# Where VectorE's share of the second weight matrix's conversion stands in a fused linear attention and gated feed-forward kernel

## The chip, the core and the metric

The kernel runs on one core of one Trainium2 chip. The core has five engines that work side by side, each through its own list of instructions in a fixed order: TensorE (PE in the profile; its weight loads are shown as PEld), VectorE (DVE), ScalarE (ACT), GpSimd (POOL) and SyncE (SP), which here issues all DMAs. An instruction waits until what it needs is there, and everything behind it on the same engine waits too. The metric is the time of one execution in microseconds on the device. The kernel before takes 837.52 us (median of 3 runs, 836.57 to 838.53).

## What is computed

Linear attention for 8 batches of 8 heads (576 positions, head size 64), then a gated feed-forward layer with a convolution of length 3 over the positions:

```python
def phi(x):
    proj = np.einsum('bhsd,df->bhsf', x, w_phi)
    proj = proj - np.max(np.abs(proj), axis=-1, keepdims=True)
    return np.concatenate([np.exp(proj), np.exp(-proj)], axis=-1)
q_p, k_p = (phi(q), phi(k))
kv = np.einsum('bhsf,bhsd->bhfd', k_p, v)
z = np.sum(k_p, axis=2)
num = np.einsum('bhsf,bhfd->bhsd', q_p, kv)
den = np.einsum('bhsf,bhf->bhs', q_p, z)[..., None] + 1e-06
x = num / den                                  # the heads side by side: 512 columns
h = np.maximum(x @ w_in, 0.0)                  # 512 x 1024
conv_out += conv_w[k][None, None, :] * hp[:, k:k + S, :]
gate = 1.0 / (1.0 + np.exp(-conv_out))
return (h * gate @ w_out).astype(np.float32)   # 1024 x 512
```

The inputs `w_in`, `conv_w` and `w_out` are 64-bit floats. They reach the kernel as pairs of 32-bit words and are turned into 32-bit floats on the chip.

## The kernel before

**Products in two parts.** Most matmuls work on operands split into a high part (rounded to the PE's fp32r form) and a low part (the rest), as three products: high by high, high by low, low by high. The helper `split` (L56 to L65) makes the two parts: the high part on the engine it is given, the low part by a subtraction (L65).

**The weights.** `load_weight(n)` handles tile n of 16, each 128 x 512: tiles 0 to 7 are `w_in`, 8 to 15 are `w_out`. For each, `weight_split` (L111) loads the raw words `w_r` by a DMA on SP (L120), and `float64_round` (L96) builds the 32-bit value in the temporary `w_t`: four instructions on DVE (L100, L102, L104, L107), two on ACT (L101, L106), one on POOL (L109). Then ACT makes the high part (L60) and POOL the low part (L65). `w_r` comes from a pool of two buffers with the tag `gh`, `w_t` from one of two with the tag `gl`. So tile n needs the buffers of tile n - 2, and the two parts of the gated activations, gh and gl, take the same buffers afterwards.

**Attention.** For each batch and each half of its heads (`qd`), five groups `g` of positions are worked on for k and for q. The rows of the profile follow this path: kx or qx (inputs split on POOL), kp or qp (projection on PE), km or qm (maximum) and ks or qs (difference) on DVE; for k, ke (exponentials on ACT) and kv (PE); for q, tp (transposed on PE), qe and qh (ACT), ql (DVE), nm (numerator and denominator, PE), num and dr (PSUM emptied by ACT), den and rc (reciprocal, DVE). `x_process(b, p)` then makes x for pair p of heads and half c of the positions: rb (PE spreads the reciprocals), xf (DVE), xh (ACT), xl (DVE, L65). The low part for b = 0, p = 3, c = 0 is called xl0_3_0; it is the last of the first batch's operands that the first half needs.

**Feed-forward.** Each of 16 halves n goes through `h_part` (hp on PE, L435, h on ACT), `conv_process` (c, on POOL and twice on DVE, L463; one sigmoid; a product on DVE, L471; then gh on ACT and gl on DVE) and `o_part` (op on PE, L494). The part op0_0 is the first output product: half 0, columns 0 to 127; op0_1 is the next, columns 128 to 255. Each needs gh and gl of half 0 (gh0_0 and gl0_0 hold the first half of their rows) and all eight tiles of `w_out`.

**What sets the order.** The code emits its steps from a small planner: generators that are resumed in a modelled time of their own, with `until` for what must have been emitted before. `weight_process` waits with tile 8 until x of (0, 3, 0) has been emitted. That is only the order of emission. A scheduler at build time then arranges the instructions of each engine anew, by priorities, dependences and estimated times, and may put a later one ahead where it sees the engine free. A helper `after(ins, trace)` traces a step such that each of its instructions on the engine of `ins` gets an edge to `ins`, and so can't be put ahead of it; the instructions on other engines get none.

```python
raw = sb.tile([P, 1024], I32, name=f"{name}r", tag="gh", bufs=2)
nc.sync.dma_start(out=raw, in_=src)
tmp = sb.tile([P, 2, 512], F32, name=f"{name}t", tag="gl", bufs=2)
```

Of the kernel before, what the change touches and what calls it, by code (L numbers as in the profile page):

```python
# [7 lines left out]
F32 = mybir.dt.float32  # L8
# [4 lines left out]
ALU = mybir.AluOpType  # L13
# [22 lines left out]
def kernel(  # L36
# [13 lines left out]
    nc = tc.nc  # L50
# [6 lines left out]
    def split(src, hi, lo, eng_hi, eng_lo):  # L57

        if eng_hi is nc.scalar:
            nc.scalar.activation(out=hi, in_=src, func=AF.Copy)  # L60
        elif eng_hi is nc.gpsimd:
            nc.gpsimd.tensor_scalar(out=hi, in0=src, scalar1=1.0, scalar2=0.0, op0=ALU.mult, op1=ALU.add)  # L62
        else:
            nc.vector.tensor_copy(out=hi, in_=src)
        eng_lo.tensor_tensor(out=lo, in0=src, in1=hi.bitcast(F32), op=ALU.subtract)  # L65


    def load_const(ap, shape, name):
# [7 lines left out]
    wbd_hi = cp.tile([P, 2 * F], F32R, name="wbd_hi")  # L76
    wbd_lo = cp.tile([P, 2 * F], F32R, name="wbd_lo")
    split(wbd_f, wbd_hi, wbd_lo, nc.vector, nc.vector)
    idn = load_const(ident, [P, P], "idn")

# [30 lines left out]
    def weight_split(src, n, hi, lo):  # L111

        name = f"w{n}_"
        if src.dtype == F32:
            raw = sb.tile([P, 512], F32, name=f"{name}r", tag="gh", bufs=2)
            nc.sync.dma_start(out=raw, in_=src)
            split(raw, hi, lo, nc.gpsimd, nc.gpsimd)
            return
# [3 lines that stand above are left out]
        w = tmp[:, 0, :]  # L122
        float64_round(raw, w, tmp[:, 1, :])
        split(w, hi, lo, nc.scalar, nc.gpsimd)
# [16 lines left out]
    def load_weight(n):  # L141
        if n < 8:
            c, sl = n // 2, slice((n % 2) * 512, (n % 2) * 512 + 512)
            weight_split(w_in[n], n, win_hi[c][:, sl], win_lo[c][:, sl])
        else:
            weight_split(w_out[n - 8], n, wout_hi[n - 8], wout_lo[n - 8])
# [10 lines left out]
    def pe(ns):  # L157
        return ("pe", ns)
# [4 lines left out]
    def until(*keys):  # L163
        return ("until", [k for k in keys if k is not None])

    def set_ready(key, ns=0):
        ready[key] = now[0] + ns * LAT
# [45 lines left out]
    def after(ins, trace):  # L213

        if ins is None:
            return trace()
        with tc.issue_after(ins.ins):
            return trace()
# [81 lines left out]
    den = {}  # L300
    numt = {}
    xh, xl = {}, {}

    def q_process(b, qd, g):
        j = (b * NQ + qd) * 5 + g
# [79 lines left out]
        if g == 2 or g == 4:  # L385
            spawn(x_process(b, qd * 2 + g // 2 - 1))

    def x_process(b, p):
        yield ("wait", 4000)
        qd, pr = divmod(p, 2)  # L390
        dn, nt = den[b, qd, pr], numt[b, qd, pr]
        if 4 * b + p > 0:
            yield until(("x", *divmod(4 * b + p - 1, 4), 1))
        with tc.high_priority():
            rc = sb.tile([72, 16], F32, name=f"rc{b}_{p}", tag="rc", bufs=2)
            nc.vector.tensor_scalar(out=dn, in0=dn, scalar1=1e-6, scalar2=None, op0=ALU.add)
            nc.vector.reciprocal(out=rc, in_=dn)
            rhl = [sb.tile([72, 16], F32R, name=f"rc{j}{b}_{p}", tag=f"rc{j}", bufs=2) for j in range(2)]
            split(rc, rhl[0], rhl[1], nc.vector, nc.vector)
            for j in range(2):  # L400
                for i in range(2):
                    nc.sync.dma_start(out=rr[2 * j + i : 2 * j + i + 1, :].bitcast(F32).rearrange("o (r c) -> o r c", c=16),
                                      in_=rhl[j].bitcast(F32).rearrange("(r i) c -> i r c", i=2)[i])
        yield ("wait", 4500)
        for c in range(2):
            yield until(("h", 2 * (b - 1) + c) if b > 0 else None)
            t0 = 0 if c == 0 else S - HW
            with tc.high_priority():
                rb = pg.tile([P, HW], F32, name=f"rb{b}_{p}_{c}", tag="g", bufs=4)
                nc.tensor.matmul(out=rb, lhsT=sel_r, rhs=rr[:, t0 : t0 + HW], start=True, stop=True)  # L410
                xf = sb.tile([P, HW], F32, name=f"xf{b}_{p}_{c}", tag="xf", bufs=2)
                nc.vector.tensor_tensor(out=xf, in0=nt[:, t0 : t0 + HW], in1=rb, op=ALU.mult)
                xh[b, p, c] = sb.tile([P, HW], F32R, name=f"xh{b}_{p}_{c}", tag="xh", bufs=8)
                xl[b, p, c] = sb.tile([P, HW], F32R, name=f"xl{b}_{p}_{c}", tag="xl", bufs=8)
                split(xf, xh[b, p, c], xl[b, p, c], nc.scalar, nc.vector)
            set_ready(("x", b, p, c), 2500)
            yield pe(125)

# [91 lines left out]
    def weight_process():  # L510
        for n in range(16):
            if n == 8:

                yield until(("x", 0, 3, 0))
            load_weight(n)
            yield ("wait", 4000)
            if n == 7:
                set_ready("w_in", 0)
        set_ready("w_out", 0)
# [18 lines left out]
    start = {}  # L538
    moe = [0.0, moe_process(), False, None]
    active.append([0.0, weight_process(), False, 0])  # L540

    def step(p, kind):
# [24 lines left out]
    while moe is not None or chains or active:  # L567
        while chains and sum(1 for p in active if p[2]) < WINDOW:
            b, x, g, kind = chains.pop(0)
# [3 lines left out]
            p = active[-1]  # L573
# [10 lines left out]
        if can_a and (a_first or not can_m):  # L584
            p = active[can_a[0]]
# [66 lines left out]
```

## Time and profile before

| | |
|---|---|
| median of 3 runs | 837.52 us (836.57 to 838.53) |
| the profiled execution | 838.25 us, of which 836.5 us from its first to its last instruction (the span) |
| mean granted PE clock | 0.99 of full speed |
| PE busy, share of the span | 797.7 us, 95% |
| PE weight loads | 781.0 us, 93% |
| DVE | 626.6 us, 75% |
| ACT | 572.6 us, 68% |
| POOL | 307.9 us, 37% |
| DMA | 49.19 MB, 59 GB/s on average |

Busy time is the time in which an engine has an instruction in work. The page also has the span in 40 slices of 20.9 us, with the busy share of each engine in tenths, so that 9 means 90% or more. A share over the whole span mixes stages with different limits, and the first 130 us of this kernel are unlike the rest: the weights are converted there and only attention has work for PE.

### The profile page before, as it was taken

The page shows a single profiled execution, that of the slowest core. Times are in us where ns is not written, and L with a number is a line of the kernel's source. Part 1 is how long each engine was busy: PE and PEld are TensorE (multiplying, and loading weights), DVE is VectorE, ACT ScalarE, POOL GpSimd, SP SyncE. Part 2 cuts the span into 40 slices and gives each one's busy share as a digit, 9 for nine tenths or more (in the row PEclk, how much of TensorE's full clock was granted, in tenths as well). Part 3 has the DMA queues.
Part 4 walks back from the last instruction along what each step waited for, and adds up shares of the span by engine and source line. Part 5 has one row for each costly group of instructions (what it writes and reads, how often), then busy time and mean ns, then how long its engine had stood idle before and what let it go on. Part 6 is the DMA issues. An engine that isn't in the chain of part 4 may idle for free.

```text
span 836.5 us, 18006 instructions
## 1 busy us (share of the span) xinstructions
PE 797.7 (95%) x6414; PEld 781.0 (93%) x6414; DVE 626.6 (75%) x1326; ACT 572.6 (68%) x1228; POOL 307.9 (37%) x469
## 2 busy tenths in 40 slices
PE   7888679999999999999999999999999999999998
PEld 6767579989999999999999999999999999999998
DVE  5889998899876777877677786778687776856561
ACT  4788777797767767786777867577585876744332
POOL 4657774443432433515133332434143221211110
PEclk9899999999999999999999999999999999999999
DMA  6544322111111211121121212112121100000001
GB/s 184 167 137 142 107 65 53 53 52 54 54 53 54 66 33 51 45 74 52 49 59 35 68 42 59 46 53 62 31 70 37 44 20 20 13 29 29 22 19 46
DMA packets 56337, 49.19 MB, mean 59 GB/s; under 512 B 15029, under 2 KB 54201, under 8 KB 56249
## 3 DMA queue, kind: packets, MB, share of 16 engines
q1 hardware_dynamic: 56248, 48.05, 19.8%
q8 instruction: 51, 0.84, 0.4%
q14 instruction: 38, 0.30, 0.1%
HBM read 38.14 MB, written 9.44 MB: 57 GB/s over the span
## 4 chain that ended last, share of the span: by engine, by line
PE 78%; DVE 9%; ACT 6%; DMA 3%; issue 3%; POOL 1%; SPq 0%; DVEq 0%; ACTq 0%; POOLq 0%
PE op L494 24%; PE hp L435 22%; PE nm L360 8%; PE kv L259 7%; PE tp L324 3%; PE qp L203 2%; PE qp L204 2%; PE qp L205 2%; PE kp L203 1%; PE kp L204 1%; PE kp L205 1%; PE kv L255 1%; DMA w_r<-in_w_in_dram 1%; PE nm L352 1%; PE rb L410 1%
## 5 line engine op out<-in xcount | busy, mean ns | idle before, releaser
L463 DVE SCALAR_TENSOR_TENSOR c<-h,cw,c 128x287 f32<-128x287 f32 (+1 forms) x256 | 138.6, 551 | 36.2 <-POOL c L458 34.3
L259 PE MATMUL kv<-v,ke 128*128 128x65 f32 x1024 | 161.1, 254 | 2.2 <-ACT ke L240 2.1
L259 PEld LDWEIGHTS kv<-v,ke 128*128 128x128 f32 x1024 | 155.2, 194 | 5.7 <-ACT ke L240 2.7
L435 PE MATMUL hp<-xh,win_hi 128*128 128x290 f32 x512 | 153.3, 301 | 2.9 <-ACT h L442 2.3
L458 POOL TENSOR_SCALAR c<-h,cw 128x288 f32<-128x288 f32 x128 | 76.7, 601 | 208.9 <-ACT h L442 170.9
L435 PE MATMUL hp<-xl,win_hi 128*128 128x290 f32 x512 | 153.0, 299 | 0.4 <-DVE xl L65 0.4
L435 PE MATMUL hp<-xh,win_lo 128*128 128x290 f32 x512 | 152.1, 297 | 0.0
L494 PE MATMUL op<-gh,wout_hi 128*128 128x288 f32 x512 | 152.1, 297 | 0.0
L494 PE MATMUL op<-gh,wout_lo 128*128 128x288 f32 x512 | 151.7, 296 | 0.0
L494 PE MATMUL op<-gl,wout_hi 128*128 128x288 f32 x512 | 151.6, 296 | 0.0
L62 POOL TENSOR_SCALAR kxh<-kr 128x256 fp32r<-128x256 f32 (+1 forms) x80 | 38.2, 477 | 198.5 <-PE kp L204 175.1
L65 DVE TENSOR_TENSOR ql<-qe,qh 128x512 fp32r<-128x512 f32 x112 | 81.9, 745 | 35.9 <-ACT qh L60 35.9
L435 PEld LDWEIGHTS hp<-xh,win_hi 128*128 128x128 f32 x512 | 97.2, 191 | 4.6 <-ACT h L442 3.1
L435 PEld LDWEIGHTS hp<-xl,win_hi 128*128 128x128 f32 x512 | 97.2, 190 | 1.2 <-DVE xl L65 1.2
L435 PEld LDWEIGHTS hp<-xh,win_lo 128*128 128x128 f32 x512 | 97.1, 190 | 0.0
L494 PEld LDWEIGHTS op<-gh,wout_lo 128*128 128x128 f32 x512 | 96.4, 188 | 0.0
L494 PEld LDWEIGHTS op<-gl,wout_hi 128*128 128x128 f32 x512 | 96.2, 188 | 0.0
L494 PEld LDWEIGHTS op<-gh,wout_hi 128*128 128x128 f32 x512 | 96.1, 188 | 0.0
L442 ACT ACTIVATE h<-hp 128x290 f32<-128x290 f32 x128 | 51.7, 410 | 51.9 <-PE hp L435 46.9
L378 ACT ACTIVATE dr<-nm 1x512 f32<-1x512 f32 (+1 forms) x96 | 46.3, 482 | 45.1 <-PE nm L360 23.6
L330 ACT ACTIVATE qe<-tp 128x512 f32<-128x512 f32 x112 | 61.9, 598 | 20.4 <-PE tp L324 16.5
L240 ACT ACTIVATE ke<-ks 128x512 f32<-128x512 f32 (+1 forms) x80 | 47.0, 588 | 39.1 <-DVE ks L210 38.6
(88 smaller groups left out, 2034.7 us busy)
## 6 DMA issues: line engine op xcount, KB each, us to landing
v<-in_vt_dram SPq DMA_DIRECT2D x80, 130.0 KB
out_dram<-os SPq DMA_DIRECT2D x64, 144.0 KB
qr<-in_qT_dram SPq DMA_DIRECT2D x64, 128.0 KB
kr<-in_kT_dram SPq DMA_DIRECT2D x64, 128.0 KB
w_r<-in_w_in_dram SPq DMA_DIRECT2D x8, 512.0 KB
w_r<-in_w_out_dram SPq DMA_DIRECT2D x8, 512.0 KB
rr<-rc SPq DMA_DIRECT2D x128, 2.2 KB
qr<-in_qT_dram SPq DMA_DIRECT2D x16, 64.0 KB
```

The costliest lines, as they stand in the source:

```text
L62: nc.gpsimd.tensor_scalar(out=hi, in0=src, scalar1=1.0, scalar2=0.0, op0=ALU.mult, op1=ALU.add)
L65: eng_lo.tensor_tensor(out=lo, in0=src, in1=hi.bitcast(F32), op=ALU.subtract)
L240: nc.scalar.activation(out=e[:, 0], in_=pr, func=AF.Exp)
L259: ins = nc.tensor.matmul(out=kp[i][:, s, p0 : p0 + VW], lhsT=lhsT, rhs=v[:, (2 * t + i) * VW : (2 * t + i + 1) * VW], start=False, stop=(g ...
L330: nc.scalar.activation(out=e, in_=tp.rearrange("p i t s -> p i (t s)"), func=AF.Exp, scale=1.0 - 2.0 * s)
L360: ins = after(ins, lambda: nc.tensor.matmul(out=ps[:, i, o : o + w], lhsT=w_, rhs=x_, start=(k == 0), stop=(k == 5)))
L378: nc.scalar.activation(out=dro.rearrange("o (r i c) -> o i r c", i=2, c=16), in_=ps[D : D + 1, :, o : o + w].rearrange("o i (r c) -> o i r ...
L435: nc.tensor.matmul(out=ps, lhsT=w_, rhs=x_, start=(k == 0), stop=(k == 11))
L442: nc.scalar.activation(out=hs, in_=ps, func=AF.Relu)
L458: nc.gpsimd.tensor_scalar(out=cv, in0=hs[:, o : o + TC], scalar1=cw[:, f, 1:2], scalar2=0.0, op0=ALU.mult, op1=ALU.add)
L463: nc.vector.scalar_tensor_tensor(out=cv[:, lo:hi], in0=hs[:, o + j - 1 + lo : o + j - 1 + hi], scalar=cw[:, f, j : j + 1], in1=cv[:, lo:hi ...
L494: nc.tensor.matmul(out=ps, lhsT=w_, rhs=x_, start=(k == 0), stop=(k == 23))
```

## The change

`split` returns its last instruction, the subtraction. `x_process` keeps that of each low part of x in `anchors`. `weight_process` issues tiles 8 and 9, the first two of `w_out`, through `after` with the anchor of (0, 3, 0), the instruction that makes xl0_3_0 on DVE. So the four DVE instructions of each of these two tiles may not stand ahead of xl0_3_0 on DVE. The rest of the two tiles, on ACT, POOL and SP, gets no edge; nor do tiles 10 to 15.

```diff
@@ split
-        eng_lo.tensor_tensor(out=lo, in0=src, in1=hi.bitcast(F32), op=ALU.subtract)
+        return eng_lo.tensor_tensor(out=lo, in0=src, in1=hi.bitcast(F32), op=ALU.subtract)
@@ beside xh, xl
+    anchors = {}
@@ x_process
-                split(xf, xh[b, p, c], xl[b, p, c], nc.scalar, nc.vector)
+                anchors[b, p, c] = split(xf, xh[b, p, c], xl[b, p, c], nc.scalar, nc.vector)
@@ weight_process
-            load_weight(n)
+            after(anchors[0, 3, 0] if n in (8, 9) else None, lambda: load_weight(n))
```

```python
def after(ins, trace):
    if ins is None:
        return trace()
    with tc.issue_after(ins.ins):
        return trace()
```

The scheduler arranges all engines anew with the edge in place, so the order differs from there on. In the rows below, names carry batch or half first, then the parts in the order used above (km1_0_2 is batch 1, half 0 of the heads, group 2; w8_t is the temporary of tile 8); the last number only counts tiles. Lines behind L302 are one higher in the change.

On DVE, right behind the last instruction of tile 7 (the end of `w_in`), before:

```order
L107 SCALAR_TENSOR_TENSOR w7_t_461<-w7_t_461,w7_r_459 128x512
L100 TENSOR_SCALAR w8_t_1711<-w8_r_1709 128x512
L208 TENSOR_REDUCE km1_0_1_748<-kp1_0_1_741 128x4
L210 TENSOR_TENSOR ks1_0_1_750<-kp1_0_1_741,km1_0_1_748 128x512
L396 TENSOR_SCALAR den0_0_1_499<-den0_0_1_499 72x16
L208 TENSOR_REDUCE qm0_1_3_758<-qp0_1_3_755 128x4
L102 TENSOR_SCALAR w8_t_1711<-w8_r_1709 128x512
L104 SCALAR_TENSOR_TENSOR w8_t_1711<-w8_r_1709,w8_t_1711 128x512
L397 RECIPROCAL rc0_1_934<-den0_0_1_499 72x16
L210 TENSOR_TENSOR qs0_1_3_760<-qp0_1_3_755,qm0_1_3_758 128x512
L107 SCALAR_TENSOR_TENSOR w8_t_1711<-w8_t_1711,w8_r_1709 128x512
L64 CAST rc00_1_937<-rc0_1_934 72x16
```

The same place in the change:

```order
L107 SCALAR_TENSOR_TENSOR w7_t_461<-w7_t_461,w7_r_459 128x512
L208 TENSOR_REDUCE km1_0_1_748<-kp1_0_1_741 128x4
L210 TENSOR_TENSOR ks1_0_1_750<-kp1_0_1_741,km1_0_1_748 128x512
L397 TENSOR_SCALAR den0_0_1_499<-den0_0_1_499 72x16
L208 TENSOR_REDUCE qm0_1_3_758<-qp0_1_3_755 128x4
L398 RECIPROCAL rc0_1_934<-den0_0_1_499 72x16
L210 TENSOR_TENSOR qs0_1_3_760<-qp0_1_3_755,qm0_1_3_758 128x512
L64 CAST rc00_1_937<-rc0_1_934 72x16
L65 TENSOR_TENSOR rc10_1_938<-rc0_1_934,rc00_1_937 72x16
L208 TENSOR_REDUCE km1_0_2_846<-kp1_0_2_839 128x4
L210 TENSOR_TENSOR ks1_0_2_848<-kp1_0_2_839,km1_0_2_846 128x512
L413 TENSOR_TENSOR xf0_0_0_863<-num0_0_0_494,rb0_0_0_861 128x290
```

The instructions of tiles 8 and 9 are gone from between the attention work, and xf0_0_0 follows sooner. The same holds for all rows of tiles 8 to 15 up to the anchor, 32 in all.

On DVE at the anchor, in the change (before, w14 and w15 were done by here, and no row of a weight follows):

```order
L65 TENSOR_TENSOR xl0_3_0_1459<-xf0_3_0_1456,xh0_3_0_1458 128x290
L100 TENSOR_SCALAR w8_t_1711<-w8_r_1709 128x512
L100 TENSOR_SCALAR w9_t_1803<-w9_r_1801 128x512
L210 TENSOR_TENSOR ks2_0_0_1476<-kp2_0_0_1470,km2_0_0_1474 128x256
L208 TENSOR_REDUCE qm1_1_1_1488<-qp1_1_1_1481 128x4
L208 TENSOR_REDUCE qm1_1_2_1507<-qp1_1_2_1500 128x4
L65 TENSOR_TENSOR xl0_3_1_1467<-xf0_3_1_1464,xh0_3_1_1466 128x290
L102 TENSOR_SCALAR w8_t_1711<-w8_r_1709 128x512
L104 SCALAR_TENSOR_TENSOR w8_t_1711<-w8_r_1709,w8_t_1711 128x512
L210 TENSOR_TENSOR qs1_1_1_1490<-qp1_1_1_1481,qm1_1_1_1488 128x512
L102 TENSOR_SCALAR w9_t_1803<-w9_r_1801 128x512
L104 SCALAR_TENSOR_TENSOR w9_t_1803<-w9_r_1801,w9_t_1803 128x512
```

Tiles 8 and 9 begin directly behind xl0_3_0 and go on in pairs between attention and the convolution of half 0.

On DVE ahead of the first low part of the gated activations, before:

```order
L471 TENSOR_TENSOR c0_1838<-c0_1838,h0_7_1649 128x288
L210 TENSOR_TENSOR qs2_0_2_2384<-qp2_0_2_2375,qm2_0_2_2382 128x512
L397 RECIPROCAL rc1_3_2804<-den1_1_1_1895 72x16
L65 TENSOR_TENSOR ql2_0_1_2431<-qe2_0_1_0_2432,qh2_0_1_2430 128x512
L65 TENSOR_TENSOR gl0_0_2441<-c0_1838,gh0_0_2440 128x288
L65 TENSOR_TENSOR ql2_0_1_2431<-qe2_0_1_1_2436,qh2_0_1_2430 128x512
```

and in the change, behind the last weight instruction:

```order
L65 TENSOR_TENSOR ql2_0_1_2431<-qe2_0_1_0_2432,qh2_0_1_2430 128x512
L398 RECIPROCAL rc1_3_2804<-den1_1_1_1895 72x16
L65 TENSOR_TENSOR ql2_0_1_2431<-qe2_0_1_1_2436,qh2_0_1_2430 128x512
L64 CAST rc01_3_2807<-rc1_3_2804 72x16
L208 TENSOR_REDUCE km2_1_2_2702<-kp2_1_2_2695 128x4
L65 TENSOR_TENSOR rc11_3_2808<-rc1_3_2804,rc01_3_2807 72x16
L210 TENSOR_TENSOR ks2_1_2_2704<-kp2_1_2_2695,km2_1_2_2702 128x512
L208 TENSOR_REDUCE qm2_0_3_2716<-qp2_0_3_2709 128x4
L210 TENSOR_TENSOR qs2_0_3_2718<-qp2_0_3_2709,qm2_0_3_2716 128x512
L65 TENSOR_TENSOR gl0_0_2441<-c0_1838,gh0_0_2440 128x288 x4
```

In the change the last DVE instruction of tile 15 (w15_t, L107) stands five rows ahead of the first of these rows, and seven rows of attention (the second ql2_0_1, rc, km, rc, ks, qm, qs) come ahead of gl0_0 that stood behind its first instruction before. On PE, op0_0 meets gl0_0 in the 906th matmul of the program in the change and in the 921st before; op0_1 ends with the 987th in both.

## The prediction

> **What bounds the kernel now.** I read the page's slices first, to see where TensorE (PE) is not full.
>
> ```profile
> PE   7888679999999999999999999999999999999998
> DVE  5889998899876777877677786778687776856561
> ```
>
> One slice is 20.9 us. PE is at 9 from the seventh slice on, so idle PE time lies in the first 130 us, and there VectorE (DVE) stands at 8 or 9. Next I cut the trace with the view of engines by stretches, at three instants found in the timeline. The columns are the stretch, its length, then busy time (and instructions) of PE, PE's weight loads, DVE, ACT and POOL, then the granted clock, the DMA share and GB/s.
>
> ```profile
> 61.79 0.65 DVE L100 TENSOR_SCALAR w_t<-w_r 128x512 int32<-128x512 int32 x1 [0.99 <-DMA w_r<-in_w_out_dram]
> 128.44 0.44 DVE L65 TENSOR_TENSOR xl<-xf,xh 128x290 fp32r<-128x290 f32 x1
> 177.90 0.45 DVE L65 TENSOR_TENSOR gl<-c,gh 128x288 fp32r<-128x288 f32 x1
> ...
> 61.80:128.40 66.60, 50.85 (x369) 44.70 (x367) 62.84 (x109) 53.53 (x113) 50.60 (x53) 0.95 0.35 105
> 128.40:178.30 49.90, 48.71 (x418) 48.48 (x418) 42.49 (x91) 38.97 (x83) 21.52 (x36) 0.97 0.20 53
> 200.00:300.00 100.00, 97.86 (x834) 97.28 (x833) 77.93 (x167) 72.52 (x157) 37.94 (x61) 1.00 0.20 55
> 300.00:500.00 200.00, 199.47 (x1668) 198.60 (x1667) 151.17 (x337) 144.85 (x317) 71.41 (x115) 1.00 0.18 51
> ```
>
> **Stage one** runs from DVE's first instruction on w_out (61.8 us) to the anchor, the low part of x of the first batch's last pair (128.4 us). DVE is busy 62.84 of 66.60 us and PE 50.85, so DVE sets the pace. **Stage two** runs from the anchor to the first low part of the gated activations, gl0_0 (done at 178.3 us). There PE is busy 48.71 of 49.90 us and sets the pace, with 7.4 us free on DVE. After 200 us PE is full, and a shift of PE's work at 200 us reaches the end undiminished.
>
> **The change, part by part.** First, what it takes out of stage one. These are the stretches again, of the instructions that touch w_t (DVE, ACT, POOL) and of those that touch w_r (DVE, ACT):
>
> ```profile
> 61.80:128.40 66.60, 23.95 (x32) 11.09 (x17) 27.32 (x18) 0.95 0.35 105
> ...
> 61.80:128.40 66.60, 23.95 (x32) 5.38 (x8) 0.95 0.35 105
> ```
>
> All 32 DVE instructions of the eight w_out tiles lie in stage one, 23.95 us of DVE. Only tiles 8 and 9 get the edge, but each later tile needs the buffers of the tile two before it, so all 32 follow the anchor in the new order. ACT's 11.09 + 5.38 = 16.5 us and nearly all of POOL's 27.3 us depend on them and move too. On SP the loads of tiles 10 to 15 move behind; those of 8 and 9 stay early and only land sooner than used. Left in stage one are DVE 62.84 - 23.95 = 38.9 us, ACT 37.1 and PE 50.85, so PE becomes the pace. Its idle 15.75 us, by releaser:
>
> ```profile
> PE rb L410 <- ACT num L383: 3.1, 2, 1.5
> PE rb L410 <- ACT qh L330: 2.2, 1, 2.2
> PE kp L203 <- DVE xf L412: 1.9, 1, 1.9
> PE tp L324 <- ACT num L383: 1.6, 1, 1.6
> PE kp L203 <- DVE ks L210: 1.5, 1, 1.5
> PE nm L360 <- DVE ql L65: 1.3, 1, 1.3
> PE kp L203 <- issue: 1.1, 2, 0.8
> PE tp L324 <- DVE qs L210: 1.1, 1, 1.1
> PE qp L203 <- DVE xf L412: 0.5, 1, 0.5
> PE nm L352 <- DVE ks L210: 0.5, 1, 0.5
> ```
>
> The waits on DVE come to about 7.4 us (6.8 in these rows, the rest in rows of 0.4 and less). I take them as gone, since DVE keeps only 38.9 us of work. The other 8.3 us wait mostly for ACT to empty PSUM. ACT loses 31% of its work, but PE to ACT to PE is a chain in itself, so I keep half, 4.2 us. The anchor then falls at 61.8 + 50.85 + 4.2 = 117 us in place of 128.4. The bounds are 112.7 (no wait left) and 121.0 (only DVE's waits gone). So **11 us are won ahead of the anchor**.
>
> Second, what it puts into stage two. In the new DVE order the 91 instructions from the anchor to gl0_0 (42.49 us) are joined by all 32 of the weights, and by seven of attention that stood behind gl0_0 before. Those seven by the groups of stage two (mean ns behind the comma):
>
> ```profile
> L65 DVE TENSOR_TENSOR ql<-qe,qh 128x512 fp32r<-128x512 f32 x10 | 7.7, 774 | 1.1 <-ACT qh L60 1.1
> L210 DVE TENSOR_TENSOR ks<-kp,km 128x512 f32<-128x512 f32 x6 | 4.1, 680 | 0.0
> L65 DVE TENSOR_TENSOR rc<-rc,rc 72x16 fp32r<-72x16 f32 x3 | 1.1, 380 | 0.0
> ```
>
> One ql, four of the ks kind (km, ks, qm, qs) and two small ones of 0.3 us give 0.77 + 4 x 0.68 + 0.6 = 4.1 us. DVE's busy time from the anchor to gl0_0 becomes 42.5 + 24.0 + 4.1 = 70.5 us. Two terms aren't in the trace. **Idle time of DVE within its order**: 7.4 us there now, when DVE was not the pace, 3.8 in stage one, when it was. Bounds 0 and 7.4; I take 4, near the stage where DVE set the pace. **Collisions with POOL**: DVE instructions last longer in stage one (POOL 50.60 us busy) than in stage two. For each, the row of stage one and then that of stage two:
>
> ```profile
> L396 DVE TENSOR_SCALAR den<-den 72x16 f32<-72x16 f32 x4 | 2.7, 684 | 0.0
> L65 DVE TENSOR_TENSOR kvl<-kvf,kvh 128x260 fp32r<-128x260 f32 x2 | 2.4, 1180 | 0.0
> ...
> L65 DVE TENSOR_TENSOR kvl<-kvf,kvh 128x260 fp32r<-128x260 f32 x4 | 2.1, 554 | 0.0
> L396 DVE TENSOR_SCALAR den<-den 72x16 f32<-72x16 f32 x3 | 0.5, 161 | 0.8 <-DMA den<-dr 0.8
> ```
>
> The four den and two kvl alone cost 4 x 0.52 + 2 x 0.63 = 3.4 us extra in stage one. POOL's weight work comes along, so some of this appears in stage two; bounds 0 and 5.4 (3.4 plus an estimated 2.0 for the smaller groups), and I take 2. The first gl0_0 is then ready 70.5 + 4 + 2 = 76.5 us behind the anchor, at 117 + 76.5 = **193.5 us, against 178.3**.
>
> Third, what PE makes of it. PE now reaches the first matmul with gl0_0 at 192.19 us, long after gl is ready; the second row is the last matmul of op0_1:
>
> ```profile
> 192.19 0.29 PE L494 MATMUL op<-gl,wout_hi 128*128 128x288 f32 x1
> ...
> 201.10 0.29 PE L494 MATMUL op<-gh,wout_lo 128*128 128x288 f32 x1
> ```
>
> In both orders the last matmul of op0_1 is the 987th of the program. Before, 66 matmuls lead to it from the first use of gl0_0, 0.135 us each. In the change gl0_0 is used 15 places earlier, so 81 x 0.135 = 10.9 us lead to it: 193.5 + 10.9 = 204.4 us against 201.1. **The 13.9 us of slack that gl0_0 had (178.3 to 192.19) are used up, and PE is 3.3 us late at 200 us.** The profiled execution took 838.25 us, which gives 841.5. It lies 0.73 above the median of the runs, 837.52, so the forecast as a median is **840.8 us**. In short, DVE has the same work to do before the first output product in either order, and what it doesn't do while waiting for PE in stage one it must do later, with PE waiting.
>
> Ends: with the anchor at 112.7, no idle, no collision and the 32 at their shortest (17.3 us, below), gl0_0 comes at 112.7 + 63.9 = 176.6 and the sum is -13.6 us. With 121.0, 7.4 and 5.4 it is +14.1 us.
>
> **The rivals.** *The relief goes through (not slower).* DVE reads as slowed by POOL in stage one. If the 32 run near their shortest behind the anchor, where POOL has more free time, DVE catches up. The rows give shortest, median and longest:
>
> ```profile
> L100 DVE TENSOR_SCALAR w_t<-w_r x16: 412/442/1372, 15.5 to 111.6; 128x512 int32<-128x512 int32 x16
> L102 DVE TENSOR_SCALAR w_t<-w_r x16: 408/506/1435, 18.4 to 116.4; 128x512 int32<-128x512 int32 x16
> L104 DVE SCALAR_TENSOR_TENSOR w_t<-w_r,w_t x16: 673/684/1769, 18.7 to 116.8; 128x512 int32<-128x512 int32 x16
> L107 DVE SCALAR_TENSOR_TENSOR w_t<-w_t,w_r x16: 674/678/1762, 21.0 to 120.3; 128x512 f32<-128x512 int32 x16
> ```
>
> Eight tiles of 0.412 + 0.408 + 0.673 + 0.674 are 17.3 us, 6.6 less, so the sum is -3.3 us and the median 834.2. It decides from a mean of 645 ns for the 32 ((23.95 - 3.3) / 32), against 748 now. For it: the medians lie near the shortest. Against: POOL's 27.3 us of the same tiles move along. The Trainium skill ("Perfetto Trace Analysis", Optimization Strategy) says that where the most-contended engine changes over time, mixing such stages can help; here that means DVE work out of DVE's stage into PE's, which is this rival. Against it stands "SBUF — State Buffer", Who interferes with whom: a VectorE instruction with two SBUF inputs and a GpSimd one that reads SBUF shut each other out for a whole instruction. The kvl rows agree; by that rule the collisions follow POOL's work and the 23.95 us stay. Chance 0.30.
>
> *Balance.* An anchor at 113.7 us, or 3.3 us less between it and gl0_0, makes 837.5. Chance 0.22.
>
> *A chain through the buffers (slower still).* gl0_0 takes the buffer of tile 14's temporary, which DVE, POOL, ACT and POOL again must finish, and four gh stand before that ACT step in ACT's new order. If this holds DVE for 4 us more, the time is 845. Nothing of the trace shows it, since the tiles were done 55 us ahead of gl. Chance 0.12.
>
> *The change doesn't do what it says.* All 32 rows stand behind the anchor in the new order; no chance is given.
>
> **How the numbers follow.** The forecast (DVE late for gl0_0 by 2 to 6 us) has 0.36. Slower by over 0.2% (1.7 us, about what can be told from no change) is 0.36 + 0.12 = 0.48, within it 0.22, faster 0.30. The range leaves out about 0.10 below 831 (anchor near its bound together with short weights) and 0.08 above 848 (the buffer chain with collisions).
>
> **What would show it.** Right: the anchor at 113 to 121 us; DVE near full from there to gl0_0, at 190 us or later; PE, full there now, with 8 us or more of waits for DVE or for gh and gl; from 300 us on no difference. Wrong: the 32 with a mean under 645 ns, or gl0_0 ready before 190 us; or the anchor hardly earlier, because PE's waits in stage one were latency. DVE also leaves this stage with less lead than before, which its free 22% from 200 to 300 us should absorb; a second stall there would add to the loss.

## The result and the profile after

The change makes the kernel slower. Four runs have a median of 844.24 us (843.77 to 845.78), beside 837.83 us for the kernel before: 1.0081 of it (95% interval 1.0063 to 1.0100). Run again on another occasion the ratio was 1.0088 (1.0073 to 1.0103). The forecast was 840.8 us, slower with a chance of 0.48, range 831 to 848. The profiled execution took 843.84 us, with a span of 842.1 us against 836.5.

The slices of the page, PE and DVE:

```profile
PE   7889998879899999999999999999999999999998
DVE  5886789989887877777778686787777776766561
```

PE is now full from the fourth slice to the sixth, where it stood at 8, 6 and 7 before, and has new dips from the seventh to the ninth and at the eleventh. To see how much each stretch wins and loses, the next two fences show the view by stretches of the kernel before and then of the change: stretch, length, busy time (instructions) of PE, weight loads, DVE, ACT and POOL, then the granted clock, the DMA share and GB/s.

```profile
62.00:112.00 50.00, 38.48 (x268) 33.37 (x267) 47.80 (x82) 41.17 (x87) 38.63 (x40) 0.93 0.40 123
112.00:150.00 38.00, 33.77 (x277) 32.73 (x278) 31.88 (x63) 27.64 (x62) 21.05 (x30) 0.96 0.19 51
150.00:190.00 40.00, 38.30 (x325) 37.37 (x324) 36.82 (x80) 33.26 (x74) 20.52 (x31) 1.00 0.18 49
190.00:230.00 40.00, 40.00 (x342) 40.00 (x341) 34.84 (x74) 30.47 (x67) 15.17 (x24) 1.00 0.20 56
230.00:300.00 70.00, 67.86 (x579) 67.28 (x578) 53.02 (x115) 49.49 (x105) 25.85 (x42) 1.00 0.20 55
```

```profile
62.00:112.00 50.00, 46.32 (x376) 42.39 (x375) 35.93 (x77) 39.64 (x90) 21.68 (x38) 1.00 0.28 77
112.00:150.00 38.00, 34.71 (x290) 33.74 (x288) 38.00 (x62) 26.54 (x59) 31.94 (x32) 1.00 0.31 92
150.00:190.00 40.00, 32.31 (x230) 29.86 (x229) 36.41 (x73) 35.26 (x74) 23.26 (x25) 0.87 0.22 64
190.00:230.00 40.00, 36.43 (x280) 35.67 (x279) 34.61 (x79) 26.18 (x54) 16.90 (x27) 0.91 0.16 48
230.00:300.00 70.00, 68.54 (x589) 67.82 (x588) 57.06 (x117) 52.61 (x115) 27.19 (x45) 1.00 0.21 59
300.00:500.00 200.00, 197.65 (x1655) 196.21 (x1654) 149.74 (x331) 142.29 (x308) 73.05 (x115) 1.00 0.19 52
```

PE loses time in two ways: it stands idle, and it works at a lower clock. A ledger of both is length minus busy time, plus length times (1 - clock):

| stretch, us | before | change | difference |
|---|---|---|---|
| 62 to 112 | 11.5 + 3.5 = 15.0 | 3.7 + 0 = 3.7 | -11.3 |
| 112 to 150 | 4.2 + 1.5 = 5.7 | 3.3 + 0 = 3.3 | -2.4 |
| 150 to 190 | 1.7 + 0 = 1.7 | 7.7 + 5.2 = 12.9 | +11.2 |
| 190 to 230 | 0 | 3.6 + 3.6 = 7.2 | +7.2 |
| 230 to 300 | 2.1 | 1.5 | -0.6 |
| 300 to 500 | 0.5 | 2.4 | +1.8 |

The sum is +5.9 us, beside 5.6 us of difference between the spans; the stretches outside the table differ by under 1 us. The account is rough: for another execution of the change (e12 below) it gives +9.4 us from 62 to 500 us beside 7.0 us of spans. So the relief of the first stage is there and large, 13.7 us, and it is given back twice: between 150 and 190 us, and between 190 and 230 us. At 190 us the change is still 2.5 us ahead by this ledger. The last matmul of op0_1, at 201.10 us before, says the same. In the change's timeline the anchor, gl0_0 and that matmul are these rows:

```profile
111.74 1.03 DVE L65 TENSOR_TENSOR xl<-xf,xh 128x290 fp32r<-128x290 f32 x1
...
187.45 1.82 DVE L65 TENSOR_TENSOR gl<-c,gh 128x288 fp32r<-128x288 f32 x4
...
198.84 0.30 PE L495 MATMUL op<-gh,wout_lo 128*128 128x288 f32 x1
```

The anchor is 16.7 us earlier, the first gl0_0 about 9.6 us later (178.3 to 187.9), and the last matmul of op0_1 2.3 us **earlier**. The lead is lost behind that matmul. PE's waits from 150 to 230 us in the change (what it waited for, sum, count, longest):

```profile
PE tp L325 <- DVE qs L210: 3.5, 2, 3.2
PE rb L411 <- ACT num L384: 2.9, 1, 2.9
PE rb L411 <- DVE ks L210: 1.8, 1, 1.8
PE nm L353 <- DVE ks L210: 1.6, 1, 1.6
```

The wait of 3.2 us ends at 180.4 us, that of 2.9 us at 214.2 us. The second one in the timelines of PE, ACT and DVE:

```profile
214.22 0.61 PE L411 MATMUL rb<-rr,sel_r 128*128 128x290 f32 x1 [2.93 <-ACT num L384]
215.31 0.61 PE L436 MATMUL hp<-xh,win_hi 128*128 128x290 f32 x1 [0.49 <-ACT os L500]
...
202.85 1.28 ACT L468 ACT_TABLE_LOAD   x1
205.87 2.13 ACT L468 ACTIVATE c<-c 128x2304 f32<-128x2304 f32 x1 [1.73 <-DVE c L464]
208.02 1.28 ACT L331 ACT_TABLE_LOAD   x1
209.31 1.09 ACT L331 ACTIVATE qe<-tp 128x512 f32<-128x512 f32 x2
...
213.40 0.77 ACT L384 ACTIVATE num<-nm 64x256 f32<-64x256 f32 x2
...
205.33 0.50 DVE L464 SCALAR_TENSOR_TENSOR c<-h,cw,c 128x287 f32<-128x287 f32 x1
```

Read from the bottom: DVE finishes the last convolution step of half 1 at 205.8 us. ACT has the sigmoid of half 1 next in its list and waits 1.73 us for that step. Behind it in ACT's list stand a table load, two exponentials qe, two qh, four gh and then the num that empties the PSUM buffer which the next rb needs, so PE stands 2.93 us. Before, the same sigmoid ran at 199.95 us and PE waited for nothing there. Of the 5.9 us by which the sigmoid is later, 1.73 us are the wait for DVE; ACT began the table load ahead of it 4.2 us later already (202.85, before 198.66). Without the 1.73 us, and with the same lists, PE would by an estimate from these rows still have stood 1.2 us (2.93 - 1.73).

### The profile page after: what moved, and what is told of

It is laid out like the page before. It is cut to its first block, busy times and chain, and to the rows that moved or that the text cites. A ratio compares the mean times of both kernels' runs of the same rounds, so it can differ in the third digit from the quotient of the medians.

```text
span 842.1 us, 17985 instructions
## 1 busy us (share of the span) xinstructions
PE 801.7 (95%) x6414; PEld 782.8 (93%) x6414; DVE 630.2 (75%) x1326; ACT 572.6 (68%) x1228; POOL 320.0 (38%) x469
## 4 chain that ended last, share of the span: by engine, by line
PE 69%; ACT 10%; DVE 10%; issue 4%; DMA 3%; POOL 3%; SPq 0%; POOLq 0%; DVEq 0%; ACTq 0%
PE op L495 19%; PE hp L436 19%; PE kv L259 7%; PE nm L361 7%; PE nm L353 3%; PE tp L325 3%; DVE c L464 2%; PE qp L203 2%; DVE ql L65 1%; DMA kr<-in_kT_dram 1%; ACT num L384 1%; ACT qe L331 1%; PE kv L255 1%; PE kp L203 1%; PE qp L204 1%
## 5 line engine op out<-in xcount | busy, mean ns | idle before, releaser
L464 DVE SCALAR_TENSOR_TENSOR c<-h,cw,c 128x287 f32<-128x287 f32 (+1 forms) x256 | 141.2, 561 | 42.8 <-POOL c L459 41.1
L459 POOL TENSOR_SCALAR c<-h,cw 128x288 f32<-128x288 f32 x128 | 83.1, 652 | 212.2 <-ACT h L443 169.0
L65 DVE TENSOR_TENSOR ql<-qe,qh 128x512 fp32r<-128x512 f32 x112 | 80.0, 734 | 39.9 <-ACT qh L60 39.9
L62 POOL TENSOR_SCALAR kxh<-kr 128x256 fp32r<-128x256 f32 (+1 forms) x80 | 40.4, 505 | 172.7 <-PE kp L204 165.1
L472 DVE TENSOR_TENSOR c<-c,h 128x288 f32<-128x288 f32 x128 | 49.1, 455 | 31.9 <-ACT c L468 31.9
```

The source lines that it names most:

```text
L65: return eng_lo.tensor_tensor(out=lo, in0=src, in1=hi.bitcast(F32), op=ALU.subtract)
L459: nc.gpsimd.tensor_scalar(out=cv, in0=hs[:, o : o + TC], scalar1=cw[:, f, 1:2], scalar2=0.0, op0=ALU.mult, op1=ALU.add)
L464: nc.vector.scalar_tensor_tensor(out=cv[:, lo:hi], in0=hs[:, o + j - 1 + lo : o + j - 1 + hi], scalar=cw[:, f, j : j + 1], in1=cv[:, lo:hi ...
L472: nc.vector.tensor_tensor(out=c4[:, f, :], in0=c4[:, f, :], in1=hs[:, o : o + TC], op=ALU.mult)
```

## The experiments

Two theories were set against each other first. **A**: DVE is the pace from 61.8 us to the last convolution step of half 1, and what it doesn't do while it waits for PE in the first stage is paid there. **B**: any new edge makes the scheduler arrange everything anew, and this arrangement is merely worse. Other rivals came up on the way (C to F, named in the expectations). All ratios are to the kernel before, run in the same rounds. An edit makes the scheduler arrange the lists anew, so most runs show an edit and a new order together. Two are free of this: e12 has the lists of the change, and e8 those of e1 less two table loads.

| run | what | median, us | ratio (95% interval) |
|---|---|---|---|
| e1_tiles14 | edge on tiles 14, 15 | 841.98 | 1.0040 (1.0027 to 1.0052) |
| e2_tiles12 | edge on tiles 12, 13 | 837.37 | 0.9992 (0.9979 to 1.0005) |
| e7_tiles10 | edge on tiles 10, 11 | 837.77 | 1.0007 (0.9995 to 1.0020) |
| e12_change_again | the change, edge on 8, 9 | 845.24 | 1.0088 (1.0073 to 1.0103) |
| e3_taps_after | change, two steps of half 1 left out | 838.59 | 1.0000 (0.9989 to 1.0012) |
| e4_taps_before | before, the same left out | 838.63 | 1.0000 (0.9988 to 1.0012) |
| e5_no_vector | before, no DVE work on w_out | 826.89 | 0.9873 (0.9858 to 0.9887) |
| e6_half_after | change, half the DVE work on w_out | 832.69 | 0.9950 (0.9934 to 0.9965) |
| e9_no_scaling | change, no POOL product on w_out | 832.14 | 0.9936 (0.9924 to 0.9947) |
| e8_tiles14_copy | e1 without two table loads | 838.45 | 1.0006 (0.9997 to 1.0015) |
| e10_anchor_0_1 | all tiles, anchor of pair 1 | 841.88 | 1.0053 (1.0039 to 1.0066) |
| e11_anchor_0_0 | all tiles, anchor of pair 0 | 846.46 | 1.0107 (1.0094 to 1.0120) |

### Is the second stall the loss?

```diff
@@ conv_process, in the change (e3) and in the kernel before (e4)
-            for j in (0, 2):
+            for j in (0, 2) if n != 1 else ():
```

Without half 1's two DVE steps, the sigmoid has nothing on DVE to wait for.

> The change, with the two VectorE steps of half 1's convolution left out (16 instructions of about 0.43 us, 7 us; half 1's output is not the reference's). Theory A (the sigmoid of half 1 on ScalarE waits for the last of them, what stands behind it on ScalarE frees PE's buffers late, and PE stands 3.4 us and then runs at a lower clock up to 220 us): the wait of 2.9 us at 214 us and the slow matmuls behind it go, 837 to 839.5, 5 to 7 below the change. Rival C (the loss is the late gl0_0 at 188 us and the cold matmuls from 180 us on, or it lies behind 300 us): within 1.5 us of the change, 842.5 to 845.5.

> The kernel before, with the same 16 steps left out (half 1's output is not the reference's). Theory A: before, PE is full from 178 us on and doesn't wait for that sigmoid, so nothing or up to 1.5 us is won: 836 to 838. If leaving them out is worth 5 us here as well, the steps cost that in any order and theory A doesn't explain the difference between the two kernels: 831 to 833.

The change comes down to the time of before (1.0000), and before doesn't move. The stretch of the second stall in e3:

```profile
190.00:230.00 40.00, 38.12 (x330) 37.59 (x328) 32.63 (x74) 30.95 (x67) 20.68 (x30) 1.00 0.22 63
```

PE's ledger there is 1.9 us in place of 7.2, the clock stays full, and the sigmoid runs at 199.60 us. The wait of 3.2 us at 180 us and the low clock behind it are still there in e3, at 181.8 us. So the first stall alone leaves the kernel level with before, and the loss lies in what comes behind it.

What of it is the wait for DVE isn't settled, because e3 has another order there. By the times of the change, its lists are the same up to 194.5 us on DVE, 195.2 us on ACT and 199.9 us on PE, and differ from there on. On ACT, behind the sigmoid of half 1, e3 has:

```profile
199.60 2.13 ACT L468 ACTIVATE c<-c 128x2304 f32<-128x2304 f32 x1 [0.31 <-POOL c L459]
201.76 0.59 ACT L379 ACTIVATE dr<-nm 1x512 f32<-1x512 f32 x1
202.37 0.77 ACT L384 ACTIVATE num<-nm 64x256 f32<-64x256 f32 x2
...
203.59 1.28 ACT L331 ACT_TABLE_LOAD   x1
```

Here num, which frees a PSUM buffer, stands right behind the sigmoid, where the change has the table load, qe, qh and gh first. The order behind 195 us makes the difference between the two kernels; DVE's late step may be one part of it and the place of num in ACT's list another, and no run has the one without the other. e4 has a new order from 185 us on as well.

### Does it come again?

> The change itself, on the chip and in the rounds of the runs beside it: 1.006 to 1.010 of before by all theories; its profile shows whether the waits of about 3 us at 180 and at 214 us, and half the clock behind each, come in another execution as well (theory A: both waits do, since the order makes them; the stretch at half the clock may shift by some us).

PE's two largest waits from 60 to 230 us in this execution:

```profile
PE tp L325 <- DVE qs L210: 4.9, 3, 3.2
PE rb L411 <- ACT num L384: 3.0, 1, 3.0
```

They end at 182.0 and 215.8 us. Both stalls belong to the order and not to one execution.

### What is there to be won?

```diff
@@ float64_round, for the tiles of w_out (before)
+        if not vector:
+            nc.scalar.activation(out=poweri, in_=high, func=AF.Relu, scale=8.0, bias=bias_e)
+            nc.scalar.activation(out=w, in_=low.bitcast(U32), func=AF.Copy, scale=2.0**-52)
+            nc.gpsimd.tensor_tensor(out=w, in0=w, in1=power, op=ALU.mult)
+            return
```

> The kernel before with VectorE's four instructions left out for the eight tiles of w_out (ScalarE's, GpSimd's and the DMAs' share stays in kind and number; the values of w_out are not the reference's). It prices the most that any move of them can bring, with nothing to pay back. Theory A (VectorE's 23.95 us hold PE in stage one and are paid back by PE later in the change): PE's idle time and low clock from 62 to 150 us (20.8 us before) fall to about 7, and nothing comes behind, so 824 to 829. Rival D (PE's waits in stage one are latency of the chain over ScalarE, and any new order loses as much elsewhere): 834 or more.

The time fell into theory A's range: DVE's work on w_out is worth 1.27%, some 10.6 us, when it is gone for good. By this a move could hardly bring more, though e5's order is new too. The path was less neat than expected: from 62 to 150 us PE's ledger fell from 20.7 to 13.5 us and not to 7.

```profile
62.00:112.00 50.00, 42.27 (x298) 37.84 (x298) 33.40 (x62) 45.60 (x98) 39.62 (x50) 0.90 0.40 126
112.00:150.00 38.00, 37.27 (x337) 37.06 (x337) 31.28 (x68) 28.38 (x64) 16.79 (x28) 1.00 0.23 62
```

### Is it the amount that is moved?

```diff
@@ weight_process (e1; e2 has (12, 13), e7 has (10, 11))
-            after(anchors[0, 3, 0] if n in (8, 9) else None, lambda: load_weight(n))
+            after(anchors[0, 3, 0] if n in (14, 15) else None, lambda: load_weight(n))
```

> The edge is put on tiles 14 and 15 alone, so 8 of the 32 VectorE instructions go behind the anchor, about 6 us. Theory A (VectorE is the pace from 61.8 us to the last convolution step of half 1, 199.5 us before and 205.8 in the change; the same 126 us of work lie there in both, and each us that VectorE idles longer while it waits for PE in stage one is paid there): with 56.8 us left VectorE stays near full in stage one, its idle time up to that step stays at 11.5 us or below, and PE's waits for it in stage one shrink, so 833 to 837, not slower than before. Theory B (any new edge makes the scheduler arrange everything anew, and the arrangement of after is merely worse): 840 to 845, with no relation to how much is moved.

> The edge is put on tiles 12 and 13, so tiles 12 to 15, 16 of the 32 VectorE instructions, go behind the anchor, about 11 us. Theory A: 50.8 us are left to VectorE in stage one beside PE's 50.85, so it idles more than with 8 moved and less than with 32; idle time up to the last convolution step of half 1 of 11 to 14 us in place of 17.7, that step at 198 to 202 us, and 835 to 840, between the run with 8 and the change. Theory B: 840 to 845.

> The edge is put on tiles 10 and 11, so 24 of the 32 VectorE instructions go behind the anchor. Theory A (what is moved is a debt, and the time grows with it once VectorE has no idle time left to pay it): between the run with 16 moved (837.4) and the change (844.2), 839 to 843. Theory B (each new order has its own stalls, unrelated to the amount): anything from 836 to 846, below 837.4 as likely as not.

With 8, 16, 24 and 32 instructions behind the anchor the ratios are 1.0040, 0.9992, 1.0007 and 1.0088. Theory A was wrong for 8 (slower, where it had the safest gain) and for 24 (no loss). For 16 it had the right time but not the path: it put half 1's last convolution step at 198 to 202 us, and that step ended at 183.6 us. So the time doesn't grow with the amount. In e2 and e7 the sigmoid of half 1 waits for DVE too (1.50 and 1.87 us), at 183.6 and 196.5 us, and PE doesn't stand more than 1.1 us at a time in the 20 us behind it: whether that wait costs anything depends on what PE and ACT have in their lists at that time.

### What made the smallest move slower?

```diff
@@ conv_process, with the edge on tiles 14 and 15
-        nc.scalar.activation(out=c4, in_=c4, func=AF.Sigmoid)
+        nc.scalar.activation(out=c4, in_=c4, func=AF.Sigmoid if n > 0 else AF.Copy)
```

> The edge on tiles 14 and 15, as in the first run, with the sigmoid of half 0 made a copy (half 0's output is not the reference's): ScalarE's order stays the same but for the two loads of its function table around it, 2 x 1.28 us, that go. Theory E (the first run lost its 4 us to the block of sigmoid, table loads and gh on ScalarE at 160 to 171 us, behind which PE's buffers came free late, with waits of 0.97 and 2.44 us and 6.9 us at half the clock behind them): those waits shrink by 2 us or more and the clock stays up, 836 to 839.5. If the loss of the first run lies elsewhere: 840.5 to 842.5.

PE's longest waits from 160 to 180 us, in e1 and then in e8 (one of 0.8 us is in both):

```profile
PE rb L411 <- ACT qh L331: 2.4, 1, 2.4
PE rb L411 <- ACT qe L331: 1.0, 1, 1.0
```

```profile
PE rb L411 <- ACT qh L331: 1.5, 1, 1.5
```

Two table loads less on ACT (2.6 us) take 1.9 us off these waits, about the 2 us expected, and 0.34% off the time (1.0040 to 1.0006). The lists are otherwise the same, so theory E holds for where the loss sits: the block of sigmoid, table loads and gh on ACT, behind which PE's buffers come free. That the clock would stay up was wrong, it stood at 0.91 of full speed from 150 to 190 us in both.

### What sets the length of stage two?

```diff
@@ float64_round, for the tiles of w_out, in the change (e6)
-        nc.vector.tensor_scalar(out=wi, in0=high, scalar1=0xFFFFF, scalar2=0x100000, ...)
-        nc.vector.scalar_tensor_tensor(out=poweri, in0=high, scalar=-2147483648, in1=poweri, ...)
@@ float64_round, for the tiles of w_out, in the change (e9)
-        nc.gpsimd.tensor_tensor(out=w, in0=w, in1=power, op=ALU.mult)
```

> The change with two of the four VectorE instructions (the mantissa's and the sign's) left out for the eight tiles of w_out, so 16 of the 32 that stand behind the anchor, about 10 us (the values of w_out are not the reference's). Theory A: the waits of 3.2 us at 180 us and 2.9 us at 214 us and the low clock behind both go, since 10 us is more than either; 12 us of idle time and low clock are to be had, so 832 to 837. Rival D: another stall takes their place, 840 or more.

> The change with GpSimd's multiplication left out for the eight tiles of w_out (8 instructions of 1.5 us; the values of w_out are not the reference's); VectorE's work stays whole. Theory F (the tiles behind the anchor are a serial chain through two buffers, over VectorE, ScalarE, GpSimd, ScalarE and GpSimd, 74.8 us for four pairs from 112.7 us to the last wout_lo at 187.5, and its length holds back the first output product and gl): each pair gets at least 3 us shorter, the last wout_lo comes at 176 us or earlier, and the time at 836 to 840. Theory A (VectorE's work alone decides): the last wout_lo stays at 183 us or later and the time within 1.5 us of the change, 842.5 to 845.5.

The low parts of w_out on POOL, with shortest, median and longest in ns, and the start of the first and of the last one: before, the change, e6, e9.

```profile
L65 POOL TENSOR_TENSOR wout_lo<-w_t,wout_hi x8: 1279/1584/2122, 70.1 to 123.5; 128x512 fp32r<-128x512 f32 x8
```

```profile
L65 POOL TENSOR_TENSOR wout_lo<-w_t,wout_hi x8: 1283/1390/1739, 124.3 to 186.2; 128x512 fp32r<-128x512 f32 x8
```

```profile
L65 POOL TENSOR_TENSOR wout_lo<-w_t,wout_hi x8: 1276/1403/1733, 120.0 to 170.3; 128x512 fp32r<-128x512 f32 x8
```

```profile
L65 POOL TENSOR_TENSOR wout_lo<-w_t,wout_hi x8: 1290/1502/1727, 122.8 to 177.0; 128x512 fp32r<-128x512 f32 x8
```

In the change the eighth low part ends at 186.2 + 1.3 = 187.5 us, and gl0_0 starts at 187.45. The low part is not what held it, though: DVE came to gl0_0 without a wait, from attention work for which it had stood 1.5 and 1.0 us, for PE's kp and qp.

In e9 DVE does all its work (its 32 instructions take 19.8 us, beside 19.9), and yet the last low part starts 9.2 us earlier and the kernel is 1.5% faster than the change (0.9936 beside 1.0088). That speaks against theory A in its plain form, that DVE's amount of work decides. It fits theory F: eight tiles that pass in turn through DVE, ACT and POOL, on two buffers, take 62 us from the first low part to the last, against 53 before, and the first output product and half 1's convolution come behind them in the lists. But it doesn't show F. The gain was larger than F's 836 to 840, e9 takes 12 us of work off POOL, and with that other DVE instructions get shorter as well: a ql between the anchor and gl0_0 takes 794 ns on average, beside 1053 in the change. The kernel before without the same POOL products, which would tell what they cost in any order, wasn't run, nor was a chain with more buffers, the direct test; e6 has no such counterpart either. In e6 the waits at 180 and 214 us are gone as well; other waits of 3.4 us at 128.6 and 2.4 us at 164.3 us came, at a lower sum.

### Would an earlier anchor be better?

```diff
@@ weight_process (e10; e11 has anchors[0, 0, 0])
-            after(anchors[0, 3, 0] if n in (8, 9) else None, lambda: load_weight(n))
+            after(anchors[0, 1, 0] if n in (8, 9) else None, lambda: load_weight(n))
```

> All tiles of w_out behind an earlier anchor, the low part of x of pair 1 in place of pair 3, with 24 of the 32 VectorE instructions still ahead of pair 3's. Theory A and F: part of the relief of stage one without the late end of the chain (last wout_lo at 150 to 162 us, 15 us or more ahead of its use) and with half 1's sigmoid not held up by VectorE: 834 to 838, not slower than before. Theory B (an edge costs by the new order): 840 or more.

> All tiles behind the anchor of pair 0, only 14 rows later on VectorE than before at the first tile and 15 at the last. Theory A and F: as before or slightly less, 835 to 839. Theory B: 840 or more.

Theories A and F were wrong here, and B's figure was right. In e10 the last low part starts at 152.7 us, as expected and 33 us earlier than in the change, and the kernel is slower than before all the same. In e11 the first instruction of tile 8 stands 14 rows later on DVE than before and the last of tile 15 stands 15 rows later, and it is the slowest of all, 1.0107. Most of its loss lies in one stretch: from 112 to 150 us its ledger is 7.5 + 4.9 = 12.4 us, beside 5.7 before. In e10 PE stands 5.7 us at 100 us, but from 62 to 150 us its ledger is only 1.9 us longer than before (22.6 us); from 150 to 190 us it is 2.6 + 3.6 = 6.2 us, beside 1.7.

```profile
100.03 0.58 PE L203 MATMUL kp<-wbd_hi,kxh 128*128 128x256 f32 x1 [5.74 <-DVE ks L210]
```

```profile
112.00:150.00 38.00, 30.54 (x232) 28.64 (x231) 33.41 (x61) 25.05 (x56) 27.58 (x30) 0.87 0.24 71
```

Which rows of the new orders make these stalls was not followed further. None of the kernels that do the whole computation beat the one before. Theories A and F each failed a forecast of their own, and theory B, that each new order has stalls of its own, is excluded by no run.

## Why the prediction was right and where it was wrong

**The direction was right, the path to it only in part, and the number came with luck.** The prediction said that DVE has the same work to do in either order and that "what it doesn't do while waiting for PE in stage one it must do later, with PE waiting". It must, and PE waits: from the anchor to gl0_0 DVE was busy for 95% of the time and PE stood 8.1 us for it. But the place and the price were wrong. With the measured anchor the prediction's own sum gives 111.7 + 76.5 + 10.9 = 199.1 us, 2.0 us earlier than before, and a median of 835.5 us: faster. An anchor that was put too late stood in for a loss behind 200 us that the sum had at nothing. So the time came out only 3.4 us above the forecast by two errors of opposite sign. One of the prediction's signs of being wrong came true outright, gl0_0 ready before 190 us, and another in one of two executions of the change, the mean of the 32 under 645 ns.

**Anchor at 117 us, at the earliest 112.7.** It came at 111.7. The waits kept for this, 4.2 us, were about right in size: PE's idle time is 49.90 - 46.22 = 3.7 us.

```profile
61.80:111.70 49.90, 46.22 (x375) 42.29 (x374) 35.83 (x77) 39.54 (x90) 21.59 (x37) 1.00 0.28 77
```

They were not the waits that the step kept, though: its rows are nearly all waits for DVE, and those for ACT, half of which were kept, come to 0.5 us. What was mis-sized is PE's own work, 46.2 us in place of 50.85. The step carried over a busy time that held stretches at half the clock: the clock was at 0.95 in that stage before (66.6 x 0.05 = 3.3 us) and at 1.00 after.

**76.5 us from the anchor to gl0_0.** Measured 76.2, the best term of all, though its parts were off against each other. The stretch of these 76 us, of instructions that touch w_t (DVE, ACT, POOL):

```profile
111.70:188.00 76.30, 19.92 (x32) 10.54 (x16) 24.01 (x16) 0.93 0.26 78
```

The 32 took 19.92 us, not 24.0. Their mean of 622 ns lies under the 645 at which the rival "the relief goes through" decides; in e12, with the same lists, they took 21.2 us, 663 ns, which is above it. The rest of DVE's work was 52.8 us (72.7 less 19.9) in place of 46.6. These rows show where the 6 us went: first before, between the anchor and gl0_0 (the prediction has 774 ns for ql there and 554 for kvl), then the change.

```profile
L463 DVE SCALAR_TENSOR_TENSOR c<-h,cw,c 128x288 f32<-128x288 f32 x8 | 4.4, 559 | 0.1
```

```profile
L65 DVE TENSOR_TENSOR ql<-qe,qh 128x512 fp32r<-128x512 f32 x10 | 10.4, 1053 | 0.0
L464 DVE SCALAR_TENSOR_TENSOR c<-h,cw,c 128x288 f32<-128x288 f32 x8 | 6.1, 772 | 0.0
L65 DVE TENSOR_TENSOR kvl<-kvf,kvh 128x260 fp32r<-128x260 f32 x4 | 3.3, 819 | 0.0
```

The Trainium skill's rule that the prediction set against the rival ("SBUF — State Buffer", Who interferes with whom) would have the collisions follow POOL's work, and so the 23.95 us stay. In sum the trace agrees: POOL was busy for 55 us of this stretch, against 21.5 us of 49.9 before, and DVE's 72.7 us are some 2 us above the 70.5 without collisions, which is the prediction's term of 2. But they fell on ql, c and kvl, which read two tiles in SBUF, more than on the 32; qs, whose qp lies in PSUM, kept its 0.68 us. That POOL is the cause is read from these rows, and from e9's shorter ql with less work on POOL; no run tests it alone. So a mean of the 32 couldn't tell whether the relief goes through. DVE's idle time was 3.6 us, as taken.

**gl0_0 at 193.5 us, PE 3.3 us late at 200 us.** This step failed. gl0_0 came at 187.9, earlier by what the anchor was early, and PE was 2.3 us early at its last matmul of op0_1. Up to here the rival of the relief had it right.

**"After 200 us PE is full", and DVE's free 22% absorbs the lead it lost.** This is the step that decided. DVE's last convolution step of half 1 was 6.3 us later (205.8, before 199.5). The sigmoid behind it came 5.9 us later, and PE stood at 211 to 214 us, long before any free time of DVE from 230 us on could help. The prediction named it at its end, as "a second stall there would add to the loss", and gave it no price. The stretch was worth 7.2 us of the ledger, more than the whole loss, and e3, without that stall, is level with before. How much of the 7.2 us DVE's lateness makes and how much the new order of ACT's list stays open.

**No difference from 300 us on.** Nearly: 1.8 us more waits from 300 to 500 us.

**The chain through the buffers (845 us, chance 0.12).** Its time was the closest, but DVE wasn't held by it: it was busy for 95% of stage two. What the chain may have done, as far as e6 and e9 tell, is to set when w_out was whole; e10, with an early end of it, was slower than before all the same.

## What to carry to other kernels

Moving work off a saturated engine is a loan, and the first to ask for it back may be a third engine: follow every in-order list behind the new position up to the next instruction that joins several engines (here a sigmoid over the whole half), and price the stall there. What a relieved stage wins can be lost at such places: here 13.7 us were won and 18.4 us given back. A busy time that is carried over from a profile carries its stretches at a low clock along. And an edge on two tiles reorders everything behind them, so a trend over the amount moved needs several points before it is believed (8, 16, 24 and 32 gave slower, same, same, slower), and an experiment that takes out a wait shows that wait alone only when the lists around it are the same.

## What the runs showed of the hardware

**Waits cost twice, by the phase of the clock.** After some waits PE runs at half its clock, for 3.4 or 6.8 us (for 10.2 us in e10, from 95.5 us). In the change this begins at 152.3, 179.6 and 213.7 us; the distances are 27.3 and 34.1 us, 8 and 10 times 3.41 us, so it follows a grid that doesn't care when the wait began. Two pairs of stretches of the change, on that grid, and one of the kernel before:

```profile
176.10:179.50 3.40, 1.08 (x12) 0.76 (x9) 3.40 (x5) 3.29 (x12) 2.53 (x2) 1.00 0.17 44
179.60:186.40 6.80, 5.99 (x30) 6.02 (x30) 4.36 (x11) 4.71 (x12) 2.86 (x6) 0.50 0.07 19
210.30:213.70 3.40, 0.98 (x8) 0.74 (x6) 3.40 (x9) 3.35 (x9) 0.00 (x0) 1.00 0.22 69
213.70:220.50 6.80, 5.80 (x24) 5.47 (x25) 5.55 (x15) 4.00 (x11) 1.70 (x3) 0.50 0.08 23
```

```profile
70.10:73.50 3.40, 1.24 (x8) 1.06 (x9) 3.40 (x5) 3.20 (x7) 3.37 (x3) 1.00 0.50 137
73.50:76.90 3.40, 3.40 (x13) 2.83 (x12) 3.40 (x7) 3.06 (x7) 2.52 (x6) 0.50 0.52 182
```

Each of these stretches at half the clock follows one in which PE was busy for 1.0 to 1.2 of 3.4 us; in three more cases of the two kernels it was 0.7 to 1.6 us. In every other window of the grid that the two kernels ran at full clock, between 60 and 830 us, PE was busy for 1.75 us or more, and the clock stayed full behind it. A wait of 2.9 us so costs up to 3.4 us more (6.8 at half the clock). The Trainium skill ("TensorE: Matmul & The Clock Gate", Part 1: The HAM clock gate) has a window of 4096 cycles, 3413 ns, that runs free of the kernel, and throttling after at least one idle window. The trace agrees on the grid; it differs on the idle window, since here windows with PE busy for up to 1.6 of 3.4 us were enough.

**The same program spreads from run to run.** The kernel before took 835.69 to 840.70 us in 29 runs of one series, with mean granted clocks from 0.982 to 0.990, and e2 834.81 to 840.17 us. The clock tells a part of it at most: e2's fastest run had 0.992 and its slowest 0.984, but the fastest of the 29 had 0.986, in the middle of them. Differences of 0.2% need many runs here.
